# Two memsets moved within the opening order, and the last expert's output product made in two column parts

## The chip, the cores and the metric

The kernel runs on one core of one Trainium2 chip. The metric is device time in microseconds (us). A core has five engines, each with a queue of its own that it works through in order: TensorE (PE, with its weight loads shown apart as PEld), VectorE (DVE), ScalarE (ACT), GpSimd (POOL) and SyncE (SP, which here issues DMAs only). They wait for one another through semaphores.

## The reference

Two stages follow each other. The first is a gated linear attention over 4 sequences, 8 heads, 768 steps and a head width of 48:

```python
f = 1.0 / (1.0 + np.exp(-f_logit))
for t in range(S):
    state = f[:, :, t, :, None] * state + np.einsum('bhd,bhe->bhde', k[:, :, t], v[:, :, t])
    y[:, :, t] = np.einsum('bhd,bhde->bhe', q[:, :, t], state)
```

Its output, reordered to 3072 tokens of 384 numbers, goes to a mixture of 16 experts (4 groups of 4). Each token picks the best group, then the best expert in it, and gets one result:

```python
h = np.maximum(xg[mask_e] @ w1[g, e], 0.0)      # 384 -> 1024
ye = h @ w2[g, e]                               # 1024 -> 384
out[tok_idx] = combined[:, None] * ye           # product of the two softmax weights
```

## The kernel before, in words

**Order.** PE, DVE, ACT and SP run in the order in which the program is written (`manual_schedule`, L85); only POOL's order is left to a scheduler. So moving a statement in the Python code moves its instruction in the queue of its engine, and nothing else.

**The attention stage.** The sequence is cut into 6 chunks of 128 steps, and each chunk into two units of two sequences, so there are 12 units. For a unit, f_logit, q, k and v are loaded (`load`, L584). The steps that matter here have one letter each:

- c, `bounded` (L593, recorded at L597): DVE clamps f_logit.
- g, `gated` (L600): ACT takes exp and log (L607, L610), PE sums over time with a triangular matrix (cs, L616), ACT makes the factors eq and kh from it (L617, L618). This runs once for each of the two sequences of a unit.
- m, `multiplied` (L630): DVE multiplies q by eq (L636) and kh by k (L639). For unit 0 the order is q of the first sequence, q of the second, k of the first, k of the second.
- t, `turned` (L642): PE transposes the products four pairs of heads at a time (tr_q and tr_k, L650), ACT copies them out of PSUM (Tq and Tk, L651).
- s, w, n, d, x: scores, weighted sums, states, gate logits and the rows of the attention's output.

The order of these steps in the first three units is written out by hand in the string `BEGIN` (L843). Two of its letters call generators that spread preparatory work over the opening. The letter p calls `padded` (L545), which sets the unused columns 48 to 63 of the head tiles, and also the tiles `other` and `gw`. The letter h calls `turn_gates` (L119): first 20 small PE transposes of the gates' weights into PSUM (L123), and at the next h four DVE copies of them into `gw` (L127). One call of p is made before the string starts, so the order of the opening is

```python
BEGIN = """c0 g0 p g0 g0 m0 m0 m0 m0 l2 t0 t0 t0 t0 h c1 g1 g1 s0 s0 s0 s0 g1 g1 p w0 w0 n0 m1 m1 m1 m1 l3 h x0 x0 x0
```

The p of n = 1 lies ahead of the first products (m0), that of n = 2 behind the first scores (s0). `other` is written by `crossed` (L663) from the fourth unit on; `gw` is read by the gate logits (`done`, L760, matmuls at L770).

**The expert stage.** The 16 experts are worked through in passes of a fixed width. A pass gathers its tokens with an indirect DMA (`fetch`, L399), makes h from w1 (`up`, L443: matmuls at L450, the Relu on ACT at L451), and the output from w2 (`down`, L476). Most passes are 174 to 230 tokens wide and make the output with w2 as the stationary side (L486), then turn it. A pass of exactly 128 tokens, as the last one is, goes through `down_rows` (L467): eight matmuls at L471 add up a tile of 128 tokens x 384 columns in one PSUM bank, with h as the stationary side and w2 as the moving one. `put` (L454) then scales the rows on ACT (L458) with a factor that differs from partition to partition, and issues the indirect DMA that scatters them to the output on POOL (L461). The last pass is called at L999. Nothing follows it but a check of two flags, whose branches are not taken here, and the closing semaphores.

**PSUM.** Tiles from `bank` (L80) rotate through 7 banks. A new tile waits until the earlier use of its bank is over.

Of the kernel before, what the change touches and what calls it, by code (L numbers as in the profile page):

```python
# [10 lines left out]
FP32 = mybir.dt.float32  # L11
# [3 lines left out]
AF = mybir.ActivationFunctionType  # L15
# [3 lines left out]
P = 128  # L19
# [4 lines left out]
def kernel(  # L24
# [12 lines left out]
    nc = tc.nc  # L37
    B, H, S, D = q.shape
    N, DM = out.shape
# [3 lines left out]
    GE = G * EG  # L43
# [5 lines left out]
    FO = F // P  # L49
# [27 lines left out]
    def const(shape, dtype, name):  # L77
        return cp.tile(shape, dtype, tag=name, name=name)

    def bank(shape, name):  # L80
        return ps.tile(shape, FP32, tag="bank", name=name)
# [30 lines left out]
    gw = const([P, 2, HP, 32], FP32, "gw")  # L112
# [6 lines left out]
    def turn_gates():  # L119
        pt = bank([D, G + 1, 4, H], "gw_ps")  # L120
        for g in range(G + 1):
            for e in range(4):
                nc.tensor.transpose(out=pt[:, g, e, :], in_=gates[:, g, :, e], identity=ident[0:H, 0:H])  # L123
        yield
        for h in range(2):
            for b in range(2):
                nc.vector.tensor_copy(gw[DP * h:DP * h + D, b, :, 0:NL], pt.rearrange("d g e (a r) -> d r a (g e)", r=2)[:, h ^ b])  # L127
        yield
# [28 lines left out]
    def constants():  # L157

        nc.vector.tensor_scalar(parti[:, :, :, 0], rowi, 6, None, OP.logical_shift_right)
        nc.vector.tensor_scalar(parti[:, :, :, 1], rowi, 63, None, OP.bitwise_and)  # L160
        nc.vector.tensor_copy(part, parti)
        nc.vector.tensor_copy(partb, parti)
        nc.vector.memset(halves, 0.0)
        nc.vector.memset(halves[0:64, 0:1], 1.0)
        nc.vector.memset(halves[64:128, 1:2], 1.0)
        restart()
# [228 lines left out]
    def load_weights(pool, ap):  # L395
        e = value(ap, GE - 1)
        return load_layer(pool, e, 1), load_layer(pool, e, 2)

    def fetch(pool, rows, n, top=N, late=False):  # L399

        w = {"n": n, "pool": pool, "early": top < N, "late": late, "blocks": [(j, min(P, n - j * P)) for j in range((n + P - 1) // P)]}
        w["x"] = pool.tile([P, len(w["blocks"]), RW], FP32, tag="xg", bufs=2 if pool is ep else 6, name="xg")
        for j, m in w["blocks"]:
            nc.gpsimd.indirect_dma_start(out=w["x"][:, j, :], out_offset=None, in_=x_dram[0:1 + top, :], in_offset=bass.IndirectOffsetOnAxis(ap=rows[:, j:j + 1], axis=0))  # L404
        return w
# [48 lines left out]
    def put(w, j, m, yp):  # L454

        y = w["pool"].tile([P, DM], FP32, tag="yt", bufs=2 if w["pool"] is ep else 4, name="yt")
        if w["n"] == P or "rows" in w:
            nc.scalar.activation(y[0:m], yp[0:m], AF.Copy, scale=w["x"][0:m, j, DM:DM + 1])  # L458
        else:
            nc.vector.tensor_scalar(y[0:m], yp[0:m], w["x"][0:m, j, DM:DM + 1], None, OP.mult)  # L460
        sent = nc.gpsimd.indirect_dma_start(out=out, out_offset=bass.IndirectOffsetOnAxis(ap=w["x"][0:m, j, DM + 1:RW].bitcast(U32), axis=0), in_=y[0:m], in_offset=None, bounds_check=N - 1, oob_is_err=False)  # L461
        if not w["late"]:

            tc.declare_no_dep(sent.ins, group="outputs", reason="each pass has rows of its own")
            tc.add_to_no_dep_group("outputs", sent.ins)

    def down_rows(w, w2):  # L467

        yp = bank([P, DM], "yo")
        for fo in range(FO):  # L470
            nc.tensor.matmul(yp, lhsT=w["h"][:, fo, :], rhs=w2[:, fo, :], start=(fo == 0), stop=(fo == FO - 1))  # L471
            if fo == FO - 4:
                yield
        put(w, 0, P, yp)

    def down(w, w2):  # L476
        n = w["n"]
        if n == P:
            for _ in down_rows(w, w2):
                pass  # L480
            return
        w["yT"] = w["yT_full"][:, :, 0:n]
        for m in range(KO):
            yp = bank([P, n], "yo")
            for fo in range(FO):
                nc.tensor.matmul(yp, lhsT=w2[:, fo, m * P:(m + 1) * P], rhs=w["h"][:, fo, :], start=(fo == 0), stop=(fo == FO - 1))  # L486
            nc.scalar.copy(w["yT"][:, m, :], yp)  # L487

    def scaled(w, settle=False):
        if w["n"] > P:  # L490
            for j, m in w["blocks"]:
                with settled(settle and j):
                    put(w, j, m, w["rows"][:, j, :])
# [16 lines left out]
    def turn_out_block(w, j, m):  # L510
        pt = bank([P, DM], "y_ps")
        for k_ in range(KO):
            nc.tensor.transpose(out=pt[0:m, k_ * P:(k_ + 1) * P], in_=w["yT"][:, k_, j * P:j * P + m], identity=ident)
        put(w, j, m, pt)
# [15 lines left out]
    with ExitStack() as fast:  # L530
# [14 lines left out]
        def padded():  # L545

            for n in range(4):
                for nm in ("eq", "qh", "kh", "v"):
                    if n < len(pads[nm]):
                        nc.vector.memset(pads[nm][n][:, :, :, D:DP], 1.0 if nm == "eq" else 0.0)  # L550
                if n == 1:
                    for t in sum(states, []):
                        nc.vector.memset(t[:, :, :, D:DP], 0.0)
                    nc.vector.memset(other[:, :, D:DP], 0.0)
                    nc.vector.memset(gw, 0.0)
                if n < 3:
                    yield
            constants()
            yield
# [298 lines left out]
        def step(nm, i):  # L858
# [12 lines left out]
            elif 0 <= i < NU:  # L871
# [9 lines left out]
                next(steps_of[nm, i], None)  # L881

        pad, turning = padded(), turn_gates()
        next(pad)
        load(0, ("f", "qh", "k"))
# [27 lines left out]
    def pass_of(n):  # L913
        p = PLACES[n]
        if p < EARLY:
            return fetch(mo, rows_p[:, p, 1:2], P)
        return fetch(mo, rows_p[:, p, :], WIDTHS[p - EARLY])
# [22 lines left out]
    ws = {n: pass_of(n) for n in range(3)}  # L940
    ahead = {n: load_weights(wq if n % 3 == 1 else wp, who[0:1, PLACES[n]:PLACES[n] + 1]) for n in range(1, 2)}
# [22 lines left out]
    for n in range(GE - 1):  # L964
        w = ws[n]
# [30 lines left out]
    turn_out(ws.pop(GE - 2))  # L996
    for _ in last_up:
        pass
    down(ws[GE - 1], ahead.pop(GE - 1)[1])  # L999
    in_turn.close()  # L1000
    main.close()

# [68 lines left out]
    with tc.If(more > 0), ExitStack() as late:  # L1071
# [5 lines left out]
        with tc.For_i(0, last, 1) as i:  # L1077
            w1, w2 = load_weights(wp, b_expert[0:1, bass.ds(i, 1)])
# [13 lines left out]
            w = fetch(ep, row, P, late=True)  # L1092
# [32 lines left out]
```

## Time and profile before

| | |
|---|---|
| median of 3 runs | 410.77 us (410.62 to 410.91) |
| the profiled execution | 410.61 us |
| its span, first to last instruction | 408.82 us |
| mean granted TensorE clock | 0.999 |
| attention stage with routing, about 0 to 132 us | PE busy 10.2 us of the first 12, 119.9 of the next 120 |
| experts, 173 to 392 us | PE busy 219.0 us of 219 |
| the last 16.8 us of the span | PE busy 11.4 us, ACT 2.7, POOL 4.9 |

The page of a profile gives busy times by engine over the whole span, then groups of instructions by line, and the chain of work that ended last: followed back from the last instruction, at each step to what released it, or to the instruction before it on its engine. "issue" in a chain is time in which the engine waited for nothing that the profile shows. The order of time lists instructions merged by line, each with its start, its length, and in brackets the idle time of its engine before it and what ended that. A matmul written once in the code appears as two records, so the eight matmuls of the last output are sixteen records. Records of matmuls overlap, since a matmul's record runs from its start to its modelled end while the next one is already streaming.

### The profile page before, as it was taken

How to read it: one execution, taken by the hardware profiler on the slowest of the kernel's cores; microseconds unless marked ns; L12 is line 12 of the kernel's file. 1: busy time of each engine (PE TensorE's matmuls, PEld its weight loads, DVE VectorE, ACT ScalarE, POOL GpSimd, SP SyncE). 2: the span in 40 equal slices, each digit the busy share in tenths (PEclk: the TensorE clock that was granted, in tenths of full speed). 3: DMA queues.
4: the chain of work that ended last, by engine and by line, in shares of the span. 5: the costliest groups of instructions: out<-in, count | busy, mean ns of one | idle time of the engine just before them, and what ended most of it. 6: DMA issues, size and time to landing. Idle time of an engine off the chain costs nothing.

```text
span 408.8 us, 10274 instructions
## 1 busy us (share of the span) xinstructions
PE 401.3 (98%) x4143; PEld 369.6 (90%) x4143; DVE 264.9 (65%) x783; ACT 162.9 (40%) x365; POOL 86.0 (21%) x132
## 2 busy tenths in 40 slices
PE   8999999999999999999999999999999999999994
PEld 3888888888888969799999999999999999999992
DVE  6666887887998805601999749468576586585230
ACT  6777888888564202121312123122121222222130
POOL 5000010102040084011222123220411310120240
PEclk9999999999999999999999999999999999999999
DMA  9999988789969599993846739468487596485010
GB/s 188 204 216 211 197 176 175 149 164 270 276 214 375 198 319 331 349 326 80 311 138 246 249 135 356 138 257 296 130 327 224 175 354 227 148 314 164 28 50 22
DMA packets 132146, 88.99 MB, mean 218 GB/s; under 512 B 102582, under 2 KB 122748, under 8 KB 132090
## 3 DMA queue, kind: packets, MB, share of 16 engines
q1 hardware_dynamic: 125666, 75.50, 62.0%
q0 software_dynamic: 5792, 11.92, 9.7%
q10 hardware_dynamic: 632, 0.83, 0.6%
q8 instruction: 35, 0.57, 0.5%
q14 instruction: 21, 0.17, 0.1%
HBM read 78.71 MB, written 9.83 MB: 217 GB/s over the span
## 4 chain that ended last, share of the span: by engine, by line
PE 52%; issue 30%; DMA 8%; POOL 6%; DVE 2%; POOLq 1%; ACT 0%; SPq 0%; DVEq 0%
PE hp L450 12%; DMA out_dram<-yt,xg 7%; PE yo L486 7%; PE yo L471 4%; PE cs L616 4%; POOL out_dram L461 4%; PE x_ps L795 3%; PE tr_q L650 3%; PE tr_k L650 3%; PE y L746 3%; PE y L754 2%; PE ap L704 2%; PE ap L689 2%; POOL xg L404 2%; PE ds L722 2%
## 5 line engine op out<-in xcount | busy, mean ns | idle before, releaser
L450 PE MATMUL hp<-xe,w 128*128 128x128 f32 (+14 forms) x864 | 138.6, 320 | 0.0
L450 PEld LDWEIGHTS hp<-xe,w 128*128 128x128 f32 x864 | 135.8, 190 | 0.8
L433 DVE STREAM_TRANSPOSE yr<-yT 32x192 f32<-32x192 f32 (+1 forms) x208 | 70.5, 339 | 70.4 <-ACT yT L487 67.8
L486 PE MATMUL yo<-h,w 128*128 128x230 f32 (+13 forms) x672 | 115.8, 333 | 0.0
L486 PEld LDWEIGHTS yo<-h,w 128*128 128x128 f32 x672 | 113.7, 190 | 0.2
L451 ACT ACTIVATE h<-hp 128x256 f32<-128x256 f32 (+14 forms) x72 | 34.4, 478 | 103.6 <-PE hp L450 103.6
L426 DVE STREAM_TRANSPOSE xe<-xg 32x192 f32<-32x192 f32 (+1 forms) x208 | 69.7, 335 | 8.6 <-PE hp L450 5.6
L461 POOL DMA_INDIRECT out_dram<-yt,xg x32 | 34.5, 1078 | 148.4 <-ACT yt L458 142.8
L487 ACT COPY yT<-yo 128x230 f32<-128x230 f32 (+13 forms) x42 | 13.5, 325 | 80.5 <-PE yo L486 80.5
L404 POOL DMA_INDIRECT xg<-x_dram,rows_p x30 | 29.6, 987 | 53.5 <-DMA out_dram<-yt,xg 29.6
L623 POOL DMA_DIRECT2D ends<-eq x10 | 5.4, 542 | 79.5 <-ACT eq L617 79.5
L471 PE MATMUL yo<-w,h 128*128 128x384 f32 x64 | 21.3, 486 | 0.0
L707 DVE TENSOR_TENSOR am<-ap,tri 128x512 f32<-128x512 f32 x24 | 15.1, 692 | 6.9 <-PE ap L704 6.9
L616 PE MATMUL cs<-ld_f,tri 128*128 128x384 f32 x48 | 18.5, 505 | 0.2 <-ACT ld_f L610 0.2
L471 PEld LDWEIGHTS yo<-w,h 128*128 128x128 f32 x64 | 11.9, 190 | 7.4
L458 ACT ACTIVATE yt<-yr,xg 128x384 f32<-128x384 f32 (+13 forms) x26 | 14.4, 604 | 5.4 <-DVE yr L433 5.4
L757 ACT COPY xT<-y 128x512 f32<-128x512 f32 x24 | 13.4, 587 | 5.5 <-PE y L746 4.4
L650 PE MATMUL tr_q<-ident,qh 128*128 128x128 f32 x96 | 14.5, 273 | 0.5 <-issue 0.5
L651 ACT COPY Tk<-tr_k 128x512 f32<-128x512 f32 x24 | 14.8, 621 | 0.0
L651 ACT COPY Tq<-tr_q 128x512 f32<-128x512 f32 x24 | 14.6, 607 | 0.4 <-PE tr_q L650 0.3
L692 DVE TENSOR_TENSOR am<-ap,seen 128x384 f32<-128x384 f32 x24 | 12.2, 552 | 3.8 <-PE ap L689 3.8
L650 PE MATMUL tr_k<-ident,kh 128*128 128x128 f32 x96 | 14.3, 273 | 0.0
(187 smaller groups left out, 433.8 us busy)
## 6 DMA issues: line engine op xcount, KB each, us to landing
w<-in_moe_w_dram SPq DMA_DIRECT2D x34, 1536.0 KB, 10.9
qh<-in_q_dram SPq DMA_DIRECT2D x12, 384.0 KB, 5.0
ld_k<-in_k_dram SPq DMA_DIRECT2D x12, 384.0 KB, 5.5
v<-in_v_dram SPq DMA_DIRECT2D x12, 384.0 KB, 5.7
ld_f<-in_f_logit_dram SPq DMA_DIRECT2D x11, 384.0 KB, 5.3
x_dram<-x_kept SPq DMA_DIRECT2D x2, 1536.0 KB, 8.3
x_dram<-x POOLq DMA_DIRECT2D x2, 384.0 KB, 4.3
x_dram<-x ACTq DMA_DIRECT2D x2, 384.0 KB
```

The lines of the kernel that those rows point to most:

```text
L404: nc.gpsimd.indirect_dma_start(out=w["x"][:, j, :], out_offset=None, in_=x_dram[0:1 + top, :], in_offset=bass.IndirectOffsetOnAxis(ap=rows ...
L426: squares(w, lambda n, k_, rk, g, rg: nc.vector.transpose(out=xT[rg, 0:n, k_], in_=x[rk, 0:n, g]))
L433: squares(w, lambda n, k_, rk, g, rg: nc.vector.transpose(out=y[rk, 0:n, g], in_=yT[rg, 0:n, k_]))
L450: nc.tensor.matmul(hp[:, o, :], lhsT=w1[:, ko, (f + o) * P:(f + o + 1) * P], rhs=w["xT"][:, ko, :], start=(ko == 0), stop=(ko == KO - 1))
L451: nc.scalar.activation(h[:, f:f + 2, :], hp, AF.Relu)
L461: sent = nc.gpsimd.indirect_dma_start(out=out, out_offset=bass.IndirectOffsetOnAxis(ap=w["x"][0:m, j, DM + 1:RW].bitcast(U32), axis=0), in ...
L471: nc.tensor.matmul(yp, lhsT=w["h"][:, fo, :], rhs=w2[:, fo, :], start=(fo == 0), stop=(fo == FO - 1))
L486: nc.tensor.matmul(yp, lhsT=w2[:, fo, m * P:(m + 1) * P], rhs=w["h"][:, fo, :], start=(fo == 0), stop=(fo == FO - 1))
L616: nc.tensor.matmul(cs.rearrange("t h d -> t (h d)"), lhsT=tri, rhs=nl[:, b], start=True, stop=True)
L650: nc.tensor.transpose(out=pt[:, a, :], in_=w[nm + "h"][:, b, 2 * a:2 * a + 2, :].rearrange("t r d -> t (r d)"), identity=ident)
L651: nc.scalar.copy(w["T" + nm][:, b], pt)
L707: nc.vector.tensor_tensor(am[:, r], ap[r], tri.unsqueeze(1).broadcast_to((P, HP, P)), OP.mult)
```

## The change

The memset of `other` moves from the p of n = 1 to the p of n = 2. The memset of `gw` leaves `padded` and goes into `turn_gates`, behind the 20 transposes, so that it stands in DVE's order behind the four products of unit 0. The copies into `gw` stay where they were.

The last pass no longer calls `down` but a new function, `down_parted`. It makes the output in two parts, columns 0 to 255 and columns 256 to 383, each with eight matmuls and a PSUM bank of its own, and each scaled by an ACT instruction of its own into the same output tile. The scatter, now in a function `send`, stays one DMA of all 384 columns, issued once both parts are scaled. All other passes of `down` are as before.

```diff
@@ turn_gates
             for e in range(4):
                 nc.tensor.transpose(out=pt[:, g, e, :], in_=gates[:, g, :, e], identity=ident[0:H, 0:H])
+        nc.vector.memset(gw, 0.0)
         yield
@@ put
         else:
             nc.vector.tensor_scalar(y[0:m], yp[0:m], w["x"][0:m, j, DM:DM + 1], None, OP.mult)
+        send(w, j, m, y)
+
+    def down_parted(w, w2):
+
+        y = w["pool"].tile([P, DM], FP32, tag="yt", bufs=4, name="yt")
+        for cols in (slice(0, 2 * P), slice(2 * P, DM)):
+            yp = bank([P, cols.stop - cols.start], "yo")
+            for fo in range(FO):
+                nc.tensor.matmul(yp, lhsT=w["h"][:, fo, :], rhs=w2[:, fo, cols], start=(fo == 0), stop=(fo == FO - 1))
+            nc.scalar.activation(y[:, cols], yp, AF.Copy, scale=w["x"][:, 0, DM:DM + 1])
+        send(w, 0, P, y)
+
+    def send(w, j, m, y):
+
         sent = nc.gpsimd.indirect_dma_start(out=out, ...
@@ padded
                 if n == 1:
                     for t in sum(states, []):
                         nc.vector.memset(t[:, :, :, D:DP], 0.0)
+                if n == 2:
                     nc.vector.memset(other[:, :, D:DP], 0.0)
-                    nc.vector.memset(gw, 0.0)
@@ end of the expert stage
     for _ in last_up:
         pass
-    down(ws[GE - 1], ahead.pop(GE - 1)[1])
+    down_parted(ws[GE - 1], ahead.pop(GE - 1)[1])
```

## The prediction

> **What bounds the kernel now.** I read the page first, then the chain that ended last, then the order of time around the two places that the change touches: the first 18 us and the last 16 us.
>
> ```profile
> PE 401.3 (98%) x4143; PEld 369.6 (90%) x4143; DVE 264.9 (65%) x783; ACT 162.9 (40%) x365; POOL 86.0 (21%) x132
> ```
>
> TensorE (PE) is busy for 98% of the span, so a microsecond on any other engine counts only where PE waits for it, or before PE's first and after PE's last matmul. The change touches one place of each kind. The chain shows the opening:
>
> ```profile
> 6.43 0.91 PE cs L616 x2
> 7.34 0.51 issue
> 7.85 0.63 PE tr_q L650 x4
> 8.47 0.04 issue
> 8.51 0.66 PE tr_q L650 x4
> 9.17 0.94 PE tr_k L650 x8
> ```
>
> From 8.51 on the chain runs through PE without a break. Before it stands a hole of 0.51 us. The order of time says what sits beside that hole (columns: start, length, engine, line, operation; in brackets the idle time before it and what ended it):
>
> ```profile
> 6.89 0.17 DVE L554 MEMSET other<- 128x128 f32 x1
> 7.06 0.27 DVE L555 MEMSET gw<- 128x256 f32 x1
> 7.26 0.49 DVE L636 TENSOR_TENSOR qh<-qh,eq 128x384 f32<-128x384 f32 x1
> 7.38 0.49 ACT L617 ACTIVATE eq<-cs 128x384 f32<-128x384 f32 x1 [0.23 <-PE cs L616]
> ...
> 7.90 0.56 DVE L636 TENSOR_TENSOR qh<-qh,eq 128x384 f32<-128x384 f32 x1 [0.15 <-ACT eq L617]
> ...
> 8.51 0.42 PEld L650 LDWEIGHTS tr_q<-ident,qh 128*128 128x128 f32 x4 [0.28 <-DVE qh L636]
> ...
> 9.96 0.56 DVE L597 TENSOR_SCALAR ld_f<-ld_f 128x768 f32<-128x768 f32 x1 [0.57 <-DMA ld_f<-in_f_logit_dram]
> ```
>
> The reader is to see two products of q. The first stands right behind the two memsets. The second starts 0.03 us after ACT's second eq (7.38 + 0.49 = 7.87), with VectorE (DVE) idle for 0.15 us before it; it does not stand behind the memsets at all. PE's second group of tr_q waits for that second product. Then the other end of the kernel:
>
> ```profile
> 397.91 4.82 PEld L471 LDWEIGHTS yo<-w,h 128*128 128x128 f32 x16
> 398.02 5.33 PE L471 MATMUL yo<-w,h 128*128 128x384 f32 x16
> ...
> 403.43 0.58 ACT L458 ACTIVATE yt<-yo,xg 128x384 f32<-128x384 f32 x1 [4.83 <-PEq L1071]
> 404.29 1.00 POOL L461 DMA_INDIRECT out_dram<-yt,xg  x1 [7.04 <-ACT yt L458]
> ```
>
> Here everything is serial: PE ends at 403.35, ACT scales 384 columns until 404.01, GpSimd's (POOL) scatter starts 0.28 us later, its DMA lands 3.0 us after its start, at 407.29, and the closing semaphores end the span at 408.82. A shift of ACT's end moves the end of the span one for one.
>
> **The two memsets.** On DVE they occupy 6.89 to 7.26, 0.37 us. The first eq was ready at 6.28 + 0.48 = 6.76, and q's load, issued from 1.84 to 2.65, landed 4.3 us later, at 6.14 or, counted from the issue's end, 6.95; so the first product can start at 6.89 to 6.95, and PE's first tr_q group near 7.5 in place of 7.85. But the second product keeps its 7.90, because its eq comes from cs, ACT and the second load of f_logit, none of which the memsets touch. PE's second tr_q group keeps 8.51, and PE only waits 0.37 us more in front of it. ACT's first Tq copy moves up and finds its own wait again behind the second group. Worth on the path: 0. The bound from above is 0.37 us, if the second product moved too.
>
> Where they go: in the instruction order of the changed kernel, which was built but not run, gw stands between the second product of k and the clamp L597, and other behind the memsets of qh, kh and v of the third round, ahead of the products of the next unit. The k products end at 8.37 + 1.02 = 9.39; the clamp sits at 9.96 after 0.57 us of waiting for its load, so gw's 0.27 is covered. For other:
>
> ```profile
> 15.23 0.27 DVE L550 MEMSET v<- 128x256 f32 x1
> ...
> 15.42 0.50 DVE L636 TENSOR_TENSOR qh<-qh,eq 128x384 f32<-128x384 f32 x1
> ...
> 16.52 0.56 DVE L639 SCALAR_TENSOR_TENSOR kh<-kh,ld_k 128x384 f32<-128x384 f32 x1 [0.60 <-DMA ld_k<-in_k_dram]
> ```
>
> It pushes one q product by 0.17 to 0.20 us, and the k product behind it waits 0.60 us for its load anyway. Without these covers the costs would be 0.27 and 0.20 us on DVE, and on the path less. Neither memset issues a DMA, no wait in SP's or POOL's list of instructions changes, and the readers (gw's copies at 17.93, other's first writer several units later) come long after.
>
> **The last output in parts.** Each matmul of the code is two records of the trace. The time of one record by width comes from the chain, where 48 records stand in one piece:
>
> ```profile
> 182.61 9.32 PE yo L486 x48
> ...
> 218.21 8.68 PE yo L486 x48
> ```
>
> The first is 230 columns wide, the second 214: 0.1942 and 0.1808 us a record, so 0.833 ns a column and 2.5 ns beside them. That gives 0.3225 for 384 columns; sixteen make 5.16, and the chain has 5.16 for the same L471 at 168.45. For 256 columns it gives 0.2158, for 128 it gives 0.1092 (four tr_q records took 0.44 in the chain, 0.110 each). The change makes 16 x (0.2158 + 0.1092) = 5.20 in place of 5.16: PE ends 0.04 later.
>
> ACT then makes two scalings. The first, 256 columns, lies under the second part's 1.75 us of matmuls. The second, 128 columns, is the one on the path. No row is that scaling; the PSUM copies of ACT give the slope: 128x512 took 0.587, 128x384 took 0.478, 0.85 ns a column. So 0.580 - 256 x 0.00085 = 0.36 us, 0.22 less. The copy of 128x128 (L772, 0.27) says the same: 0.21 less than the 384 copy. Net at the end: 0.22 - 0.04 = 0.18 us gained.
>
> [...] The second part loads eight weights again, 16 more records. The row is L450: weights of 128x128 with a moving side of 128, in pieces of 48 records that took 5.44 us, 0.113 each, with PEld and PE side by side; loading is hidden down to this width. [...] by the row, 0.04 to 0.10. [...]
>
> The second part also has a wait of its own: its first matmul waits for an earlier PE write of its PSUM bank. Queued behind it are the other matmuls of the part, and ACT waits for the last. The parts of the expert before have the same wait at L486, and the timeline shows their 88 records from 378.76 as one busy piece; so 0. From above, a PE pipe run empty and filled again costs about one 128-wide record from start to end, 0.27 us. A gain there I exclude: a wait adds none.
>
> **Sum.** The profiled execution took 410.61 us, 1.79 outside its span of 408.82. 410.61 - 0 - 0.18 = 410.43. The median of the runs shown is 0.16 above it, so 410.77 - 0.18, about 410.6. A measurement of this kernel tells about 0.2%, 0.8 us, from no change; this lies within.
>
> **Rivals.**
> - Both parts pay: the second q product is after all released by the first, and the opening gives 0.37. 410.77 - 0.18 - 0.37 = 410.2. The 0.15 us of idle time that ACT ended speaks against it. 8%.
> - The seam eats the gain: 0.27 for the pipe between the parts and 0.06 for narrow records, against 0.22: 410.9. The unbroken L486 piece speaks against it. 13%.
> - Slower: the second part's weight loads lie bare, since each load is as long as the matmul it should hide under. [...] it decides against the change from about 11 ns bare for each of the 16 loads (0.18 / 16), and is told from no change at about 0.06 us each. L450 speaks against it. 5%.
> - That the memsets do nothing on the path is my forecast's own case, not a rival.
>
> **How the numbers follow.** Forecast 66%, the three rivals 8, 13 and 5; 8% are left for a knock-on in the 260 us between that nothing here names, half each way. Faster by over 0.2% is 4%, slower 5 + 4 = 9%, the rest 87% within. The range goes from 410.1, the first rival with the spread of the runs (0.15 below the median), to 411.1, the second with the same spread.
>
> **What would show it.** Right: the first qh product near 6.9, the second still at 7.9, PE's second tr_q group still at 8.5; gw's memset near 9.4 and the clamp still at its load; 16 records of 256 and 16 of 128 within 5.4 us; the last scaling 0.36 long, and the span 0.18 shorter. Wrong: the second tr_q group before 8.4, a hole in PE between the parts, records of 128 columns above 0.12 us apart, or a last scaling above 0.45.

## The result, and the profile after

The changed kernel took 411.45 us (median of 18 runs, 410.63 to 412.34); the kernel before took 410.77 beside it (18 runs, 410.55 to 411.70). The ratio is 1.0013, with a 95% interval of 1.0007 to 1.0019. The medians lie 0.68 us apart, and by the ratio the change costs about 0.5 us, where 0.18 had been forecast as a gain. The difference lies within the 0.2% that the prediction called no change, but its interval excludes equality, and 411.45 lies outside the forecast range. The runs of the changed kernel also spread wider: their standard deviation is 0.50 us, against 0.26 before.

The profiled execution of the changed kernel took 410.93 us, one of its shorter ones, with a span of 409.0. So what it shows is less than the median's loss, and the sizes are taken from the experiments' profiles as well. From its page, the span and the busy times by engine:

```profile
span 409.0 us, 10307 instructions
...
PE 401.7 (98%) x4159; PEld 371.9 (91%) x4159; DVE 264.8 (65%) x783; ACT 163.1 (40%) x366; POOL 85.9 (21%) x132
```

PE and PEld have 16 records more, ACT one more, as written. The order of time at the end of the changed kernel (start, length, engine, line, operation; in brackets the idle time before and what ended it):

```profile
398.19 5.32 PEld L470 LDWEIGHTS yo<-w,h 128*128 128x128 f32 x32
398.30 5.40 PE L470 MATMUL yo<-w,h 128*128 128x256 f32 x32
...
402.00 0.47 ACT L471 ACTIVATE yt<-yo,xg 128x256 f32<-128x256 f32 x1 [3.12 <-PE yo L470]
403.74 0.37 ACT L471 ACTIVATE yt<-yo,xg 128x128 f32<-128x128 f32 x1 [1.26 <-PE yo L470]
404.38 1.00 POOL L476 DMA_INDIRECT out_dram<-yt,xg  x1 [6.85 <-ACT yt L471]
```

The reader is to see that this part did what it was to do: 32 records in one piece of 5.40, and a last scaling of 0.37. From the first yo matmul to the start of the scatter it takes 404.38 - 398.30 = 6.08 us, against 404.29 - 398.02 = 6.27 before: 0.19 gained. And yet the span is 0.19 longer. Of that, 0.28 is that yo starts later here (398.30 against 398.02), and 0.10 is behind the scatter's start. The next lines give, for this last scatter, the time from its start on POOL to its landing: first before, then after, then in the experiment that makes the second part of the change alone (e2_parts_only):

```profile
DMA to landing us min/median/max: 3.0/3.0/3.0
```

```profile
DMA to landing us min/median/max: 3.2/3.2/3.2
```

```profile
DMA to landing us min/median/max: 4.5/4.5/4.5
```

Nothing about the scatter was changed: both profiles list 64 packets and 0.14 MB for it, on the same queue. What changed is what else moves on the DMA engines at that time. The view of the DMA queues for packets that start from 404.5 to 409.5 us (queue, kind of transfer: packets, MB, share of the 16 engines), before:

```profile
q0 software_dynamic: 64, 0.14, 7.9%
q14 instruction: 2, 0.02, 1.4%
```

and after:

```profile
q0 software_dynamic: 64, 0.14, 8.1%
q14 instruction: 2, 0.02, 1.5%
q8 instruction: 1, 0.02, 1.5%
```

q0 is the scatter. "instruction" is, by its name, program code being fetched; q8 is taken for the queue on which PE's comes, since in each of the eleven profiles with the branch below a fetch on it follows that branch on PE by 0.66 to 1.25 us, wherever the branch stands. After the change one fetch of PE's code (16,384 bytes by its packet record, 406.48 to 407.64) stands in the window of the scatter; before, the same fetch ran from 403.67 to 404.82, a microsecond before the scatter's first large packet (405.86). Its place follows from one row: the branch in PE's list of instructions that tests whether a fallback is needed. The rows of PE's sequencer at the two lines of that test (operation, count: ns min/median/max, first and last start in us), before:

```profile
L1070 PEldq TENSOR_LOAD <-both_i x1: 485/485/485, 398.7 to 398.7; - x1
...
L1071 PEldq COMPARE_BRANCH  x1: 3761/3761/3761, 399.3 to 399.3; - x1
```

and after:

```profile
L1085 PEldq TENSOR_LOAD <-both_i x1: 486/486/486, 401.3 to 401.3; - x1
...
L1086 PEldq COMPARE_BRANCH  x1: 3876/3876/3876, 401.9 to 401.9; - x1
```

The test stands 2.7 us later. Its branch takes 3.8 and 3.9 us, where the same branch takes 50 to 72 ns on the other four engines. One fetch on q8 lies inside the branch (400.22 to 401.50 before, 403.42 to 404.30 after); the one that matters is the next, which follows 0.66 to 0.67 us behind the branch's end in both. Two things are to be read here. First, the sequencer reaches the test long before PE has done the work in front of it: before at 398.66, with 14 matmul records of yo still to start, after at 401.34, with 17 left. In time that is 4.7 us of PE's work before and 2.4 after, so the lead is nearer to a number of places than to a time. Second, the change doubled the places between the start of yo and the test, from 16 records with 16 weight loads to 32 with 32, in nearly the same time of PE (5.33 and 5.40 us). If the lead is counted in places, and the last of them are now 0.11 us each and no longer 0.32, the sequencer arrives later; e5 below tests this with the same 32 records in another order.

### The profile page after: what moved, and what is told of

Its sections match the earlier page's. It is cut to its first block, busy times and chain, and to the rows that moved or that the text cites. A ratio compares the mean times of both kernels' runs of the same rounds, so it can differ in the third digit from the quotient of the medians.

```text
span 409.0 us, 10307 instructions
## 1 busy us (share of the span) xinstructions
PE 401.7 (98%) x4159; PEld 371.9 (91%) x4159; DVE 264.8 (65%) x783; ACT 163.1 (40%) x366; POOL 85.9 (21%) x132
## 4 chain that ended last, share of the span: by engine, by line
PE 53%; issue 30%; DMA 7%; POOL 6%; DVE 2%; POOLq 1%; ACT 0%; DVEq 0%
PE hp L451 12%; DMA out_dram<-yt,xg 7%; PE yo L501 7%; PE yo L486 4%; PE cs L631 4%; POOL out_dram L476 4%; PE x_ps L810 3%; PE tr_k L665 3%; PE y L761 3%; PE tr_q L665 3%; PE y L769 2%; PE ap L719 2%; PE ap L704 2%; POOL xg L405 2%; PE ds L737 2%
## 5 line engine op out<-in xcount | busy, mean ns | idle before, releaser
L486 PE MATMUL yo<-w,h 128*128 128x384 f32 x48 | 16.0, 487 | 0.0
L632 ACT ACTIVATE eq<-cs 128x384 f32<-128x384 f32 x24 | 12.5, 523 | 4.0 <-PE cs L631 3.9
```

## The experiments

The theories, as the expectations name them or mean them. M: the moved memsets make the loss. S: the output in parts makes it. C: neither; the opening is later because PE's clock rises at another moment. After the first three runs, for how the parts lose: F, the later test moves PE's code fetch onto the scatter's packets; R, two PSUM banks and two scalings cost more than the trace shows; L, a later test costs by itself, since PE then ends later. Each ratio is to the kernel before on the same chip, with its 95% interval. "Landing" is the time from the scatter's start on POOL until its DMA has landed.

**e1_memsets_only** is the kernel before with the memsets moved:

```diff
@@ turn_gates, behind the transposes
+        nc.vector.memset(gw, 0.0)
@@ padded
+                if n == 2:
                     nc.vector.memset(other[:, :, D:DP], 0.0)
-                    nc.vector.memset(gw, 0.0)
```

> The kernel before with the two memsets moved as in the change, and the last output made as before. Theory M (the memsets' new places make the opening slower): 0.5 to 1.0 us slower than before, like the whole change plus the 0.19 us that its end gains. Theory S (the two column parts make some executions slower): within 0.2 us of before. Theory C (neither edit costs: the moment at which PE's granted clock rises, 5.28 us in the profile of before and 6.45 us in that of the change, is not tied to the kernel and costs what it will): within 0.3 us of before, with a scatter like that of before run beside it.

Measured 410.83 against 410.92, ratio 0.9999 (0.9991 to 1.0007). The order of time in the opening of e1:

```profile
6.84 0.51 DVE L637 TENSOR_TENSOR qh<-qh,eq 128x384 f32<-128x384 f32 x1
...
7.46 0.63 PE L651 MATMUL tr_q<-ident,qh 128*128 128x128 f32 x4
...
7.90 0.56 DVE L637 TENSOR_TENSOR qh<-qh,eq 128x384 f32<-128x384 f32 x1 [0.55 <-ACT eq L618]
...
8.52 0.66 PE L651 MATMUL tr_q<-ident,qh 128*128 128x128 f32 x4 [0.43 <-DVE qh L637]
...
9.40 0.27 DVE L124 MEMSET gw<- 128x256 f32 x1
...
9.85 0.56 DVE L598 TENSOR_SCALAR ld_f<-ld_f 128x768 f32<-128x768 f32 x1 [0.17 <-DMA ld_f<-in_f_logit_dram]
```

The first product and the first tr_q group move up by 0.4 us, the second pair stays at 7.90 and 8.52, and PE waits 0.43 us between the groups. M falls: no cost and no gain of the memsets can be told.

**e2_parts_only** is the kernel before with the output in parts (the new functions are those of the change, and left out here):

```diff
-    down(ws[GE - 1], ahead.pop(GE - 1)[1])
+    down_parted(ws[GE - 1], ahead.pop(GE - 1)[1])
```

> The kernel before with the last output in parts of 256 and 128 columns, and the memsets where they were. Theory M: 0.15 to 0.2 us faster than before, as the end of the changed kernel's profile shows. Theory S: 0.5 to 0.9 us slower and scattered over more than 1 us, as the changed kernel was. Theory C: 0.1 to 0.2 us faster in the median.

Measured 411.72 against 410.92, ratio 1.0015 (1.0009 to 1.0022): the whole loss is here, and C, which asked for a gain, falls with M. Its profile, of one of its longest executions, is the clearest of all. PE's test, and the DMA queues from 404.5 to 409.5:

```profile
L1084 PEldq TENSOR_LOAD <-both_i x1: 485/485/485, 401.5 to 401.5; - x1
...
L1085 PEldq COMPARE_BRANCH  x1: 3536/3536/3536, 402.1 to 402.1; - x1
```

```profile
q0 software_dynamic: 64, 0.14, 8.6%
q8 instruction: 1, 0.02, 1.5%
q14 instruction: 2, 0.02, 1.0%
```

The packet records of this execution show how it comes about (start and end in us, queue, bytes; some of them):

```
406.661 407.862  q8   16384   PE's code
407.341 407.463  q0    3072   scatter, the last of its other large packets
407.848 408.182  q0    3072   scatter, behind PE's code
```

All large packets of the scatter end by 407.47 except one, which starts as the code fetch ends and itself takes 0.33 us, where others of 3,072 bytes take 0.12. The records don't name the DMA engine; that this packet shares one with the fetch, and had to wait for it, is read from the fit of the times. The landing is 4.50 us, and the span ends 1.47 behind it, as it does before (408.82 - 407.34 = 1.48). Of the 1.45 that the landing takes longer than before, 0.98 is the later end of the last large packet; the other 0.47 lies between that and the landing, and the packets give no reason for it.

**e3_change_again** is the changed kernel once more, beside e1 and e2.

> The changed kernel once more, for a second profile and to see whether the 0.7 us come back. Theories M and S: 0.5 to 0.9 us slower than before, scattered over more than 1 us. Theory C: anything from 0.2 us faster to 0.7 us slower, and the profile shows a rise of the clock near 5.3 us with a span of about 408.6, or a later one with a longer span.

Measured 411.80 against 410.92, ratio 1.0021 (1.0011 to 1.0032). The loss and the wide spread of the runs are there again. The landing is 3.53, and here no packet follows PE's fetch (406.77 to 407.76). The last ones follow a fetch on q14, which starts 2.13 us behind the scatter's start, where it was 1.61 before, and two of them, of 4,608 bytes, take 0.24 and 0.26 us beside PE's fetch, where 0.18 is usual behind a fetch. So neither profile of the changed kernel itself, both of executions faster than its median, shows what e2 shows.

**e4_one_scaling** has the two column parts of matmuls, but in one bank with one scaling:

```diff
+        yp = bank([P, DM], "yo")
         for cols in (slice(0, 2 * P), slice(2 * P, DM)):
-            yp = bank([P, cols.stop - cols.start], "yo")
             for fo in range(FO):
-                nc.tensor.matmul(yp, ...
-            nc.scalar.activation(y[:, cols], yp, AF.Copy, scale=w["x"][:, 0, DM:DM + 1])
+                nc.tensor.matmul(yp[:, cols], ...
+        nc.scalar.activation(y, yp, AF.Copy, scale=w["x"][:, 0, DM:DM + 1])
```

> The changed kernel, with both column parts in one PSUM bank and one scaling of 384 columns behind them: the second bank and the second scaling are gone, the 32 PE records stay. Theory F (the doubled number of PE records makes PE's sequencer reach the flag check 2.7 us later, and the fetch of code behind its branch then falls on the last scatter's packets): as slow as the change or slower, 0.6 to 1.1 us over before, with a fetch on queue q8 near 406.7 us and the scatter landing up to 4.5 us after its start. Rival R (two banks or two scalings make the scatter or its wait longer): as before, 0.05 us slower at most.

Measured 412.10 against 410.96, ratio 1.0026 (1.0018 to 1.0034), the slowest of all. The gain of the short scaling is gone and the loss is still there, so R falls: of the change only the added matmul records are left. PE's code runs from 406.20 to 408.02, three large scatter packets follow behind it, the first at 408.01, and the landing is 4.83.

**e5_small_part_first** makes the 128 columns first, then the 256:

```diff
-        for cols in (slice(0, 2 * P), slice(2 * P, DM)):
+        for cols in (slice(0, P), slice(P, DM)):
```

> The changed kernel with the 128 columns first and the 256 last. The records stay 32, but the last sixteen take 3.45 us in place of 1.75, so PE's sequencer is through earlier. Theory F: the check starts near 399.9, the second fetch runs from about 405.0 to 406.1, ahead of most packets; the scatter lands 3.0 to 3.2 us after its start, and the time is within 0.2 us of before (0.11 gained by a scaling of 256, 0.04 lost on PE). Rival R: as slow as the change, 0.5 to 0.9 us over before.

Measured 410.95 against 410.96, ratio 1.0000 (0.9991 to 1.0008). The records are the same 32, but those that the sequencer still has ahead of it are now the long ones. Its test and its scatter's landing:

```profile
L1085 PEldq TENSOR_LOAD <-both_i x1: 482/482/482, 399.9 to 399.9; - x1
```

```profile
DMA to landing us min/median/max: 3.3/3.3/3.3
```

So the test is reached at 399.90, again with 17 records left, and PE's code runs from 404.73 to 405.69, ahead of the scatter's large packets, which begin at 406.08. No loss is left. That no gain remains goes with the last scaling, 0.48 us in place of 0.37, which leaves 0.1 to gain.

**e6_parts_interleaved** makes the small part's first five steps, then the large part, then the small part's last three:

```diff
-        for cols in (slice(0, 2 * P), slice(2 * P, DM)):
-            yp = bank([P, cols.stop - cols.start], "yo")
-            for fo in range(FO):
+        wide, last = slice(0, 2 * P), slice(2 * P, DM)
+        banks = {c.start: bank([P, c.stop - c.start], "yo") for c in (last, wide)}
+        for cols, fos in ((last, range(5)), (wide, range(FO)), (last, range(5, FO))):
+            yp = banks[cols.start]
+            for fo in fos:
...
+            if fos.stop == FO:
```

> The changed kernel with five matmuls of the 128-column part first, then the eight of 256 columns, then the last three of 128: two banks, two scalings and 32 records as in the change, but the last 32 entries of PE's queue take 3.4 us, about as before the change. Theory F: the check starts near 400.2, the second fetch is over before or just as the scatter's packets begin, the scatter lands 3.0 to 3.2 us after its start, and the time is 0.1 to 0.2 us faster than before. Rival R: as slow as the change, 0.5 to 0.9 us over before.

Measured 411.12 against 410.96, ratio 1.0005 (0.9997 to 1.0013). It was to keep both the short scaling and an early test, and it missed. The test at 400.12 was early, but PE's code ran from 405.11 to 406.61 in its profile, longer than the 0.9 to 1.3 of most others at this place, and still into the scatter, three of whose large packets follow it; landing 3.76.

**e7_change_no_fallback** and **e8_before_no_fallback** are the changed kernel and the kernel before without the fallback. They leave out the work for data whose flags ask for more blocks, which the data here do not, and so the test, its branch and the code behind it:

```diff
-    more = nc.values_load(both[0:1, 1:2], ...
-    with tc.If(more > 0), ExitStack() as late:
...
```

> The changed kernel without the fallback stage behind the flag check: the check, its branches and the code that they jump over are left out (on these inputs that code is never entered, so the output is the same). Theory F (code fetch behind PE's branch falls on the last scatter): with no far branch there is no such fetch, the scatter lands about 3 us after its start, and the kernel is 0.1 to 0.25 us faster than the kernel before with the same cut, run beside it as e8. Rival R: 0.5 to 0.9 us slower than that one.

> The kernel before without the fallback stage, left out as in e7, as the other half of that pair. Theories F and R: within 0.5 us of the kernel before, on the faster side, since the scatter met no late fetch there and only the check itself goes.

e7 measured 409.72, ratio 0.9972 (0.9960 to 0.9983), e8 410.03, ratio 0.9982 (0.9974 to 0.9990), both against 410.87. The DMA queues of e7 at the end (404.5 to 409.0), and its scatter:

```profile
q0 software_dynamic: 64, 0.14, 8.8%
```

```profile
DMA to landing us min/median/max: 2.5/2.5/2.5
```

No code is fetched, and the landing is 2.51, in e8 2.49. The span ends 1.16 us behind the landing in both, in place of 1.48. Before e8 ran, it was expected within 0.5 us of the kernel before; it came out 0.84 below, because no fetch was thought to meet the scatter there. So even before the change the landing took 0.56 us longer (3.05 - 2.49) than without the test and its fetches: those on q14 before run at 405.10 to 405.61 and 405.90 to 406.48, and three scatter packets follow directly behind the second. And without any fetch the order of the two kernels turns: e7 is 0.31 below e8 in medians. Their two intervals overlap, so the size is not settled; the profiles give 6.08 us from the first yo matmul to the scatter's start in e7 and 6.27 in e8, so 0.19.

**e9_check_pushed_later** and **e10_check_pushed_past** go the other way: the changed kernel with 6 or 10 small matmuls behind the last part, whose result nothing uses, so that the sequencer reaches the test still later:

```diff
+        idle = bank([P, P], "idle")
+        for _ in range(10):
+            nc.tensor.matmul(idle, lhsT=onesb, rhs=onesb, start=True, stop=True)
         send(w, 0, P, y)
```

> The changed kernel with six small bf16 matmuls, whose result nobody reads, behind the last part, so that PE's sequencer reaches the flag check about 0.7 us later still, and the fetch behind its branch starts near 407.1, when the scatter's packets are nearly all through. Theory F (only the meeting of fetch and packets costs): most of the loss goes, 0.2 us faster to 0.3 us slower than before, landing 3.0 to 3.3 us. Rival L (a later check costs by itself, the later the more): 1.0 us or more slower than before.

> The changed kernel with ten small bf16 matmuls behind the last part in place of the six of e9, so that the fetch behind PE's branch starts about 3 us after the scatter, when its packets are through (2.5 to 2.7 us in the undisturbed profiles). Theory F: the 0.2 us that the parts gain become visible, 0.05 to 0.25 us faster than before, landing about 3.1 us. Rival L (a later check costs by itself): 0.3 us or more slower.

e9 measured 410.83 against 410.87, ratio 0.9999 (0.9990 to 1.0007); e10 410.63 against 410.91, ratio 0.9994 (0.9986 to 1.0003). The test in e10, and its scatter:

```profile
L1088 PEldq TENSOR_LOAD <-both_i x1: 483/483/483, 402.5 to 402.5; - x1
...
L1089 PEldq COMPARE_BRANCH  x1: 3442/3442/3442, 403.1 to 403.1; - x1
```

```profile
DMA to landing us min/median/max: 3.0/3.0/3.0
```

In e10 the code arrives from 407.77 to 408.65, behind the landing at 407.24, and the loss is gone with the latest test but the longest list of matmuls. L falls; the span also ends 1.47 to 1.48 us behind the landing in all eleven profiles with the test, early or late. In e9 the fetch (406.74 to 407.73) begins when three large packets of the scatter are left, and these end by 407.15 beside it; here too no loss can be told.

**e11_before_late_check** is the kernel before, its output in one part, with the same ten matmuls behind it:

```diff
     down(ws[GE - 1], ahead.pop(GE - 1)[1])
+    idle = bank([P, P], "idle")
+    for _ in range(10):
+        nc.tensor.matmul(idle, lhsT=onesb, rhs=onesb, start=True, stop=True)
```

> The kernel before, its last output and memsets untouched, with ten small bf16 matmuls, whose result nobody reads, behind the last output. They run after PE's last useful matmul and only take places in PE's queue, so the check starts near 401 us in place of 398.7. Theory F: the fetch behind the branch falls on the scatter as it does in the change, and the kernel is 0.5 to 1.2 us slower than before. Rival R (the parts themselves cost): no difference, within 0.15 us.

Measured 411.56 against 410.91, ratio 1.0017 (1.0011 to 1.0024). The test, the queues from 404.5 to 409.5, and the scatter's landing:

```profile
L1073 PEldq TENSOR_LOAD <-both_i x1: 482/482/482, 400.8 to 400.8; - x1
...
L1074 PEldq COMPARE_BRANCH  x1: 3716/3716/3716, 401.4 to 401.4; - x1
```

```profile
q0 software_dynamic: 64, 0.14, 8.3%
q8 instruction: 1, 0.02, 1.6%
q14 instruction: 2, 0.02, 1.4%
```

```profile
DMA to landing us min/median/max: 3.9/3.9/3.9
```

The test is reached at 400.77, PE's code runs from 405.75 to 407.06, on the scatter (large packets from 406.00 to 407.85), three of whose packets follow it, and the landing is 3.89. So the loss can be made without the change, by ten matmuls that cost nothing in e10. F stands: what counts is where the fetch falls, not how many records there are nor whether the output is made in parts.

One more rival can be settled from these profiles. The recorded clock goes from 1.0 to 0.5 at the end, at 408.1 us in the profile before, but at 405.8 to 406.6 in those of after, e2, e3, e4 and e6, while the scatter's DMA runs. In e11 it falls at 409.18, behind the landing, and the landing takes 3.89 all the same; in e9 it falls at 405.90, and the landing takes 3.37 and no loss is seen. So an early fall of the clock is neither needed for the loss nor enough for it.

## Why the prediction was wrong, point by point

- **The two memsets: right.** Worth 0, as e1 shows; the first product at 6.84 (predicted near 6.9), the second at 7.90, PE's second tr_q group at 8.52, gw's memset at 9.40 (all in e1).
- **The opening of the changed kernel's own profile** looks like a miss. Its order of time:

```profile
5.48 2.00 PE L631 MATMUL cs<-ld_f,tri 128*128 128x384 f32 x4
...
7.40 0.56 DVE L651 TENSOR_TENSOR qh<-qh,eq 128x384 f32<-128x384 f32 x1 [0.65 <-ACT eq L632]
...
8.16 0.56 DVE L651 TENSOR_TENSOR qh<-qh,eq 128x384 f32<-128x384 f32 x1 [0.21 <-ACT eq L632]
...
8.78 0.42 PEld L665 LDWEIGHTS tr_q<-ident,qh 128*128 128x128 f32 x4 [0.33 <-DVE qh L651]
```

  Both products are late, and each waits for ACT's eq, which waits for cs: it is PE that is slow here. The first two cs records start 0.77 us apart (5.48 and 6.25), in the profile before 0.40 (5.35 and 5.75). The rise of the granted clock is read from where the profile's record of it starts, with 1.0: at 6.45 us in this profile and at 5.28 in the one before; ahead of that nothing is recorded. Over all thirteen profiles it starts between 3.79 and 6.95; where that is by 5.56, the second tr_q group starts at 8.51 to 8.54, where it is from 6.40 on, at 8.74 to 8.96. It is late with the memsets in their old place (e2, 6.90; e11, 6.40) and early with them moved (e1, 4.45; e7, 3.79), so it isn't the edit. Nor is it the loss: e4, the slowest, has the opening at 8.51, and over the profiles the start of yo doesn't follow the opening (398.20 to 398.32 in e4, e5 and e7, which open early; 398.12 and 398.16 in e6 and e9, which open late).
- **PE's sum: right.** 32 records in one piece of 5.40 us; the narrow ones are 0.111 apart, and from the last wide record to the first narrow one there is no hole. From the first yo matmul to ACT's last scaling it is 5.44 us, against 5.41 before: 0.03 more, where 0.04 was predicted. The row of L450, 0.113 a record, was a good measure for these, with the weight loads (5.32 us) beside the matmuls (5.40), and the rivals of the seam and of the bare loads fall.
- **The last scaling: right.** 0.37 against 0.36 predicted. The sum of both, 0.18 gained to the start of the scatter, was 0.19.
- **The failed step** is the one behind it: "its DMA lands 3.0 us after its start", and "a shift of ACT's end moves the end of the span one for one". The 3.0 was carried over as a constant. What comes behind the landing was constant (1.47 to 1.48 us in all profiles with the test); the landing wasn't. In one profiled execution of each kernel it measured 2.5 us with no code fetch near it (e7, e8), 3.0 to 3.4 with PE's fetch ahead of it, behind it or beside its last packets (before, after, e1, e5, e9, e10), 3.5 in e3, where the fetch ran beside the last packets and these were slow, and 3.8 to 4.8 where packets of the scatter follow directly behind PE's fetch (e2, e4, e6, e11). The term that was missing is up to 1.8 us more than before (4.83 - 3.05) in one execution. For the runs as a whole it is about 0.7 to 0.9 us, an estimate: the loss of 0.5 to 0.7 and the 0.19 gained. A term that depends on the moment of the fetch goes with the wider spread of the runs (a standard deviation of 0.50 us against 0.26); whether it also depends on which DMA engine takes the fetch is not shown.
- **Why it was missed.** The 16 added records were priced as PE's time (0.04 us) and not as places in PE's queue. The description of the kernel passes over the test as "a check of two flags, whose branches are not taken here"; it is the fallback that isn't entered, while PE's sequencer spends 3.8 us at the branch and has code fetched inside it and behind it. Of steps that are moved past, the prediction looked at the lists of SP, POOL and DVE, not at what stands behind the last matmul in PE's own list. Two rows before the change told of it: COMPARE_BRANCH with 3,761 ns, and, in a line that the prediction itself shows, an idle time of ACT put down to "PEq L1071", that is to PE's sequencer at that very test. All eleven profiles with the test show a branch of 3.4 to 3.9 us with a fetch of 16,384 bytes on q8 inside it and one behind it; e7 and e8, without the test, have no such fetch near the scatter. What the branch waits for, and what the second fetch is for, is not shown; at the last transfer of this kernel, landings up to 1.8 us longer went with such a fetch.
- **The chances.** The case that held was a slowdown that no rival named; only the 8% left for what nothing names stood for it, half of it on the slower side, and it had been sought in the 260 us between, not at the end. That the difference stays within 0.2%, to which the prediction gave 87%, came true by luck: with the opposite sign, and by the size of a term that its sum hasn't got.

What stays open: why some fetches take 0.9 us and others 1.8, which DMA engine takes them, and why the fetch follows the branch's end by 0.66 to 0.68 us in eight profiles and by 1.03 to 1.25 in three (e2, e3, e10). A version with the fallback that beats the kernel before is not settled either: e10 is 0.28 us below it in medians, and its interval reaches 1.0003.

## What to carry to other kernels

An instruction added to PE costs its time there, and, as far as the sequencer's lead here is a number of places, it is also a place in a queue: 16 more matmul records in nearly the same time moved by 2.7 us the moment at which the sequencer reached the next branch, and with it the code fetch behind that branch. Where the kernel ends on a DMA, look in the view of the queues at what else moves in its window, the "instruction" queues too, and take its landing time as a result of that, not as a constant. A branch of several us in a sequencer's rows near the end (here 3.4 to 3.9) says that there may be such a fetch to place, ahead of the last transfer (e5) or behind it (e10).

## What was not expected of the hardware

- One fetch of 16,384 bytes of PE's code took 0.9 to 1.8 us, and scatter packets that look to be on the same DMA engine started only as it ended (at 407.848 for an end of 407.862 in e2, at 408.010 for 408.024 in e4).
- PE's sequencer reached the test with 14 matmul records and 13 weight loads left to start (before, e1) or 17 and 16 (the nine others with the test), for 1.6 to 4.7 us of PE's work: 27 or 33 places, as far as records are places.
- The branch over the fallback took 3.4 to 3.9 us on PE and 50 to 72 ns on the other engines.
- The moment at which the record of the granted clock starts, with 1.0, moved by 3.2 us between executions (3.79 to 6.95), and PE's second tr_q group stood up to 0.45 us later where it was late (8.96 against 8.51).
